# Attention logits from three bf16 parts instead of two fp32r parts, with the order of the stages set anew

## The chip, the cores and the metric

The kernel runs on one core of a Trainium2 chip. The metric is the device time of one execution in microseconds (us); a profiled execution of the same program gives the trace from which the views below are read. The engines are named as in the profile: PE is TensorE's matmul and PEld its weight load, DVE is VectorE, ACT is ScalarE, POOL is GpSimd, SP is SyncE, which issues most of the DMAs.

## What is computed

Two layers, each an attention with a compressive memory followed by a SwiGLU FFN, on 2048 rows of 512 numbers, in fp32. The reference, cut to the attention part that matters here:

```python
B, S, D = x.shape                      # 1, 2048, 512
H = 32; Dh = D // H; N = 4; L = S // N # 32 heads of 16, four segments of 512 rows
q, k, v = ...                          # x @ wq, x @ wk, x @ wv, as (B, H, N, L, Dh)
mask = (ar[:, None] < ar[None, :]) * (-1e9)
for s in range(N):
    qs, ks, vs = q[:, :, s], k[:, :, s], v[:, :, s]
    logits = jnp.einsum("bhqd,bhkd->bhqk", qs, ks) * scale + mask
    p = _softmax(logits, axis=-1)
    a_dot = jnp.einsum("bhqk,bhkd->bhqd", p, vs)
    ...                                # a_mem is read from M and z of the segments before
    o = g * a_mem + (1.0 - g) * a_dot
    ...                                # M and z take in this segment
return o @ wo
```

Each layer is x = x + attention(layernorm(x)), then x = x + FFN(layernorm(x)).

## The kernel before

**How the order is made.** The kernel doesn't issue as it goes. Every instruction is put on a list with its engine, an assumed cost, its readers and writers and a due time (`P.prio`), and `Program.issue` then plays the engines forward with these costs and always takes, among what is ready on an engine, what is due first. So the order on each engine's queue is fixed at build time, and on the chip each engine works its queue in that order and waits by semaphore. The constants at the top are the due times: `TA` and `TF` scale a unit of attention and a step of the FFN, `OFF` gives where within a unit each sort of work is spread, `PRE` the start of a layer, `EP`, `PAIR`, `STEP`, `WAT`, `TAT` and `FIN` the FFN.

**Precision.** A product of fp32 matrices is made from fp32r parts, high and low: three matmuls (`mm3`, line 282, for the projections) instead of one fp32 matmul of several passes. The logits do the same within one matmul: q and k have 16 numbers per head, and the three products (high by high, high by low, low by high) lie under each other in 48 rows of the contraction.

**A unit of attention** is one segment, one group of eight heads and one half of the group: four heads. There are 32 units per layer. For each unit:

- `qk_proj` (line 458, once for each tensor of a group) projects 128 columns of q or k, copies them out of PSUM (`raw`, line 468, ACT), rounds them to the high part (line 469, POOL), subtracts for the low part (line 471, POOL), and writes the parts to a scratch in DRAM with two DMAs (lines 483 and 484).
- `load3` (line 490) reads the scratch back with heads in another layout: `cq` with q's three rows of parts for each number and `ck` with k's, four DMAs of 192 KB per unit, issued by SP. Two heads lie in one contraction, in rows 0 to 47 and 64 to 111; `cq` is zero where the other head's rows are.
- `mx_units` (line 518) makes the row maxima. For each head and each block of 128 query rows one matmul of at least 256 key columns (line 531): 256 and 256 in one PSUM bank, 384 and 512 in one each; the ring of these banks, `pmx`, has two. DVE reduces each with the causal mask (line 538). A transpose (line 547), a negation (line 549, ACT) and a DMA of ACT's queue (line 550) put the negated maxima into row 127 of `cq`.
- `at_units` (line 559) makes the logits again, transposed, less the maximum: for each of ten blocks of 128 keys by 128 queries two matmuls of 256 columns (two heads each) into one bank of the ring `plt` of three (line 575); ACT takes the exponential (line 581); on the four diagonal blocks POOL zeroes the upper triangle (line 585). `pv` (line 603) multiplies by v in two steps, and `post` (from line 616) divides and writes the output.

Around these, matmuls of the projections, of the output `wo_proj`, of the memory (`mem_read`, `mem_update`) and the next segment's layernorm are spread. The FFN (lines 1005 and 1049 are its products) isn't touched except by the constants of its order.

## Time and profile before

| | us |
|---|---|
| three runs | 1931.92, 1933.54, 1934.31 |
| median of the runs | 1933.54 |
| span of the profiled execution, first to last instruction | 1931.2 |
| PE busy in the span | 1870.8 |
| DVE busy | 1406.9 |
| ACT busy | 873.0 |
| POOL busy | 905.9 |

The profiled execution has no time of its own beside its span, which lies 2.3 us under the median of the runs. A group's row reads: line, engine, operation, tiles written and read, shapes, count, then busy time, mean duration of one in ns, then the idle time of the engine just before such instructions and what ended most of it. In a timeline a row is start, duration, then the instruction. Busy time counts overlapping instructions of an engine once.

### The profile page before, as it was taken

What the parts mean: (1) busy time and instruction counts of PE and PEld (TensorE: products, weight loads), DVE (VectorE), ACT (ScalarE), POOL (GpSimd) and SP (SyncE); (2) the same over time, 40 slices, a digit from 0 to 9 for tenths busy, and PEclk for the clock granted to TensorE, in tenths of its full rate; (3) what the DMA queues carried; (4) which work ended last, traced back from release to release, by engine and by line L of the source; (5) the groups of instructions that cost most, each with busy time, mean ns of one, the idle gap of its engine ahead of it and who ended that gap; (6) DMA issues with size and microseconds to landing.
All of it is one profiled execution on the core that took longest, in us unless ns stands there. A gap on an engine that the chain in (4) does not pass through costs nothing.

```text
span 1931.2 us, 32319 instructions
## 1 busy us (share of the span) xinstructions
PE 1870.8 (97%) x11104; PEld 1437.2 (74%) x11104; DVE 1406.9 (73%) x3834; ACT 873.0 (45%) x1634; POOL 905.9 (47%) x1185
## 2 busy tenths in 40 slices
PE   7999999999989999999999999999999999999999
PEld 5677677776668887788867777777766788878887
DVE  5877867778777668766777678777797756686656
ACT  4555454555624343334326555555455334333332
POOL 5333443444546553655534334444355365455461
PEclk9999999999999999999999999999999999999999
DMA  7433434456131122221364344344561321221121
GB/s 235 135 111 124 132 116 146 129 151 195 45 136 50 55 72 82 71 61 44 95 215 121 102 133 132 116 149 132 152 188 39 131 66 44 87 77 51 44 60 44
DMA packets 120819, 206.09 MB, mean 107 GB/s; under 512 B 14160, under 2 KB 43856, under 8 KB 120656
## 3 DMA queue, kind: packets, MB, share of 16 engines
q1 hardware_dynamic: 118608, 203.49, 34.8%
q8 instruction: 89, 1.46, 0.3%
q10 hardware_dynamic: 2048, 0.53, 0.1%
q14 instruction: 74, 0.61, 0.1%
HBM read 136.34 MB, written 67.11 MB: 105 GB/s over the span
## 4 chain that ended last, share of the span: by engine, by line
PE 78%; DVE 8%; issue 4%; DMA 4%; POOL 3%; ACT 2%; SPq 0%; ACTq 0%; DVEq 0%; POOLq 0%
PE pj L282 16%; PE pj L1049 14%; PE plt L1005 11%; PE pmx L531 8%; PE pmx L1005 8%; PE ppv L603 7%; PE plt L575 6%; PE ppv L1005 3%; DVE junk L538 2%; DMA ck<-scrk 1%; PE pj L975 1%; PE pj L373 1%; PE pj L653 1%; DMA s<-nm 1%; POOL mem L858 1%
## 5 line engine op out<-in xcount | busy, mean ns | idle before, releaser
L538 DVE CUSTOM_DVE_ANT_0 junk<-pmx,amask 128x128 bf16<-128x128 f32 (+3 forms) x1024 | 458.7, 484 | 116.9 <-PE pmx L531 112.0
L282 PE MATMUL pj<-s,s 128*128 128x512 f32 x1416 | 488.2, 410 | 4.9 <-DVE s L1054 4.5
L1049 PE MATMUL pj<-s,vt 128*128 128x512 f32 x1296 | 414.4, 398 | 7.1 <-DVE s L1054 4.5
L581 ACT ACTIVATE s<-plt 128x512 f32<-128x512 f32 x512 | 284.2, 601 | 141.3 <-PE plt L575 133.3
L282 PEld LDWEIGHTS pj<-s,s 128*128 128x128 f32 x1416 | 263.9, 190 | 71.4 <-issue 24.9
L531 PE MATMUL pmx<-ck,s 127*128 127x256 f32 (+2 forms) x1024 | 299.1, 347 | 16.9 <-DVE mx L538 9.5
L1005 PE MATMUL plt<-s,s 128*128 128x512 f32 x1008 | 296.2, 396 | 3.4 <-ACT tt L1020 2.3
L1049 PEld LDWEIGHTS pj<-s,vt 128*128 128x128 f32 x1296 | 243.5, 189 | 68.9 <-DVE s L1054 8.0
L1054 DVE TENSOR_TENSOR s<-s,pj 128x512 f32<-128x512 f32 x224 | 152.9, 684 | 137.9 <-PE pj L1049 137.7
L575 PE MATMUL plt<-s,ck 128*128 128x256 f32 x1280 | 241.6, 288 | 4.2 <-DMA s<-nm 2.1
L531 PEld LDWEIGHTS pmx<-ck,s 127*128 127x128 f32 x1024 | 178.7, 190 | 88.8 <-DVE mx L538 27.0
L1005 PE MATMUL pmx<-s,s 128*128 128x512 f32 x720 | 239.2, 396 | 3.6 <-ACT s L871 2.4
L575 PEld LDWEIGHTS plt<-s,ck 128*128 128x128 f32 x1280 | 211.2, 189 | 32.7 <-ACT s L581 8.5
L1005 PEld LDWEIGHTS plt<-s,s 128*128 128x128 f32 x1008 | 189.6, 189 | 50.4 <-ACT tt L1020 2.7
L585 POOL TENSOR_SCALAR_AFFINE_SELECT s<-s 128x512 f32<-128x512 f32 x192 | 126.9, 664 | 186.5 <-ACT s L581 180.1
L1005 PEld LDWEIGHTS pmx<-s,s 128*128 128x128 f32 x720 | 135.5, 189 | 36.4 <-ACT s L871 3.2
L603 PE MATMUL ppv<-s,vt 128*32 128x512 f32 (+2 forms) x1536 | 136.8, 458 | 0.0
L872 POOL TENSOR_TENSOR s<-mem,s 128x512 fp32r<-128x512 f32 x96 | 126.4, 1318 | 0.0
L469 POOL TENSOR_SCALAR s<-raw 128x512 fp32r<-128x512 f32 x64 | 39.9, 624 | 181.0 <-ACT raw L468 180.6
L1005 PE MATMUL ppv<-s,s 128*128 128x512 f32 x288 | 112.8, 394 | 0.0
L879 POOL COPY turn<-vt 128x1 f32<-128x1 f32 x20 | 3.7, 184 | 230.0 <-DVE vt L962 230.0
L581 ACT ACTIVATE pc<-plt 128x512 f32<-128x512 f32 x128 | 76.8, 600 | 63.8 <-PE plt L575 62.5
(197 smaller groups left out, 2872.5 us busy)
## 6 DMA issues: line engine op xcount, KB each, us to landing
s<-scrq SPq DMA_DIRECT2D x128, 192.0 KB, 3.5
ck<-scrk SPq DMA_DIRECT2D x128, 192.0 KB, 4.5
scrq<-s SPq DMA_DIRECT2D x32, 512.0 KB, 3.0
scrk<-s SPq DMA_DIRECT2D x32, 512.0 KB, 3.1
scrq<-s SPq DMA_DIRECT2D x32, 256.0 KB, 2.0
scrk<-s SPq DMA_DIRECT2D x32, 256.0 KB, 2.0
xin<-xmid SPq DMA_DIRECT2D x32, 256.0 KB, 2.7
s<-xmid SPq DMA_DIRECT2D x32, 256.0 KB, 5.4
```

What stands on the lines that cost most here:

```text
L282: pe(n, passes, lambda: nc.tensor.matmul(view(ps.ap), lhsT=av(a.ap), rhs=bv(b.ap), start=start, stop=stop), [(a, rk[0]), (b, rk[1])], [ps])
L469: gp(0.59, lambda: nc.gpsimd.tensor_scalar(out=nat.ap[:, a, 0, :], in0=raw.ap, scalar1=1.0, scalar2=0.0, op0=OP.mult, op1=OP.add), [raw], ...
L531: nc.tensor.matmul(ps.ap[:, a * 256:a * 256 + nk], lhsT=cq.ap[0:127, 2 * j + p, qt * 128:(qt + 1) * 128], rhs=ck.ap[0:127, p, 0:nk], start ...
L538: dve(w, lambda a=a, qt=qt, w=w, ps=ps, junk=junk: nc.vector.tensor_tensor_reduce(out=junk.ap[:, :w], in0=ps.ap[:, a * 256:a * 256 + w], i ...
L575: nc.tensor.matmul(ps.ap[:, 256 * p:256 * p + 256], lhsT=ck.ap[:, p, kt * 128:kt * 128 + 128], rhs=cq.ap.rearrange("r (j p) c -> r p j c", ...
L581: act(512, lambda: nc.scalar.activation(Pb.ap[:, x].rearrange("p i c -> p (i c)"), ps.ap, AF.Exp, scale=SCALE), [ps], [(Pb, x)], table="exp")
L585: gp(0.593, lambda: nc.gpsimd.affine_select(out=Pb.ap[:, x], in_=Pb.ap[:, x], pattern=[[0, 4], [1, 128]], compare_op=OP.is_ge, fill=0.0, b ...
L603: nc.tensor.matmul(ps.ap[32 * i:32 * i + 32, q0:q0 + w], lhsT=vt.ap[:, kt, VW * hd:VW * hd + 32], rhs=f_[sl].ap[:, b0:b0 + w // 128, idx], ...
L872: gp(n / 400, lambda hi=hi, lo=lo, src=src: nc.gpsimd.tensor_sub(lo(), src(), hi().bitcast(F32)), [read, (wt, (o0, 0))], [(wt, (o0, 1))])
L1005: pe(512, 1, lambda i=i, kc=kc, x=x, buf=buf, view=view: nc.tensor.matmul(ps.ap, lhsT=w.ap[:, o, i, kc], rhs=view(buf.ap, kc), start=(x == 0),
L1049: pe(512, 1, lambda i=i, j=j, fi=fi, x=x, ps=ps, wt=wt, cs=cs: nc.tensor.matmul(ps.ap, lhsT=ht.ap[:, 0:2048].rearrange("p (f a c) -> p f a ...
L1054: dve(512, lambda ps=ps, t=t: nc.vector.tensor_add(xb.ap[:, t, :], xb.ap[:, t, :], ps.ap), [ps, (xb, t)], [(xb, t)])
```

## The change

q and k are each split into three bf16 parts instead of two fp32r parts: round to bf16 (POOL), subtract (POOL), round the rest (ACT), subtract again (POOL). Six products (every pair of parts but the three smallest) lie in 6 x 16 = 96 rows of the contraction, for one head per matmul; the scratch has six rows of parts, written in three DMAs, and `load3` has one DMA of 384 KB for q and one for k. The negated maximum is split into two bf16 parts as well, which go to rows 96 and 97 against rows of ones, with two DMAs. Since one head is one matmul, the columns are the exact causal widths: for the maxima 128, 256, 384 or 512 keys, packed to full banks (`MXB`, five banks for two heads); for the logits 512, 384, 256 or 128 queries (ten banks for four heads). The triangles are zeroed four heads at a time by `tri`, four instructions per unit as before, once all exponentials of the buffer's blocks are made. The planner's costs for the new matmuls count no weight load (`loads=0`). All constants of the order have new values, those of the FFN among them.

```diff
-PAIR, STEP, WAT, TAT = 13.0, 1.83, -2.5, (-1.0, -0.5)
+PAIR, STEP, WAT, TAT = 12.518, 2.534, -3.116, (-0.932, -0.425)
...
-FIN = 1.9
-WQ1 = -6.0
-TA, TF = 15.0, 16.7
-OFF = {'qe': (0.481, 1.468), 'at': (0.3, 1.1), 'mx': (-0.666, 0.16), 'lf': (-0.709, -0.318), 'mr': (0.865, 0.781), 'mu': (0.556, 0.139), 'wo': (0.263, 1.746), 'qk': (-0.342, 0.41), 'v': (-0.3, 0.518), 'lp': (0.034, 1.108)}
-PRE = {'c': -1.851, 'mb': 0.212, 'lv': -1.7, 'lo': -0.87, 'gate': -1.0, 'v': -1.534, 'dv': 0.12, 'qk1': -1.2, 'mx': -1.0}
-EP = {'w': -1.935, 'wn': 0.178, 'ln': -3.0, 'dn': -0.06, 'up': -2.73}
+FIN = 1.768
+WQ1 = -5.451
+TA, TF = 14.964, 15.962
+OFF = {'qe': (0.628, 1.66), 'at': (0.101, 1.238), 'mx': (-0.602, 0.614), 'lf': (-1.174, -1.011), 'mr': (0.951, 0.747), 'mu': (1.331, 0.736), 'wo': (-0.091, 1.887), 'qk': (0.072, 0.439), 'v': (-0.029, 1.348), 'lp': (0.034, 1.542)}
+PRE = {'c': -1.891, 'mb': -0.617, 'lv': -1.755, 'lo': -1.008, 'gate': -1.122, 'v': -1.534, 'dv': 0.401, 'qk1': -0.884, 'mx': -1.261}
+EP = {'w': -0.913, 'wn': 0.898, 'ln': -2.365, 'dn': -0.073, 'up': -4.471}
...
-                g["nat"] = sb(S8["nat"], [128, 2, 2, 512], F32R)
+                g["nat"] = sb(S8["nat"], [128, 8, 512], BF16)
...
-            gp(0.59, lambda: nc.gpsimd.tensor_scalar(out=nat.ap[:, a, 0, :], in0=raw.ap, scalar1=1.0, scalar2=0.0,
-                                                     op0=OP.mult, op1=OP.add), [raw], [(nat, (a, 0))])
-            gp(1.23, lambda: nc.gpsimd.tensor_sub(nat.ap[:, a, 1, :], raw.ap, nat.ap[:, a, 0, :].bitcast(F32)),
-               [raw, (nat, (a, 0))], [(nat, (a, 1))])
+            z = [a + (i if nm == "q" else 2 - i) for i in range(3)]
+            res = lambda: nat.ap[:, 6:8].rearrange("p a c -> p (a c)").bitcast(F32)
+            gp(0.61, lambda: nc.gpsimd.tensor_copy(nat.ap[:, z[0]], raw.ap), [raw], [(nat, z[0])])
+            gp(1.26, lambda: nc.gpsimd.tensor_sub(res(), raw.ap, nat.ap[:, z[0]]), [raw, (nat, z[0])], [(nat, "r")])
+            act(512, lambda: nc.scalar.copy(nat.ap[:, z[1]], res()), [(nat, "r")], [(nat, z[1])], sbuf=True)
+            gp(1.26, lambda: nc.gpsimd.tensor_sub(nat.ap[:, z[2]], res(), nat.ap[:, z[1]]),
+               [(nat, "r"), (nat, z[1])], [(nat, z[2])])
...
-            scr = P.buf(dram, "scr" + nm, [128, 3, 512], F32, ring=5)
-            r2, r1 = (0, 2) if nm == "q" else (1, 0)
-            dma(lambda: nc.sync.dma_start(scr.ap[:, r1], nat.ap[:, a, 0].bitcast(F32)), [(nat, (a, 0))], [(scr, r1)])
-            dma(lambda: nc.sync.dma_start(scr.ap[:, r2:r2 + 2], nat.ap[:, a].bitcast(F32)),
-                [(nat, (a, 0)), (nat, (a, 1))], [(scr, r2)], kb=512)
+            scr = P.buf(dram, "scr" + nm, [128, 6, 512], BF16, ring=5)
+            for d0, k0, k in ((5, z[0], 1), (3, min(z[:2]), 2), (0, a, 3)):
+                dma(lambda d0=d0, k0=k0, k=k: nc.sync.dma_start(scr.ap[:, d0:d0 + k], nat.ap[:, k0:k0 + k]),
+                    [(nat, e) for e in range(k0, k0 + k)], [(scr, d0)], kb=128 * k)
...
-                cq = sb(S8[f"c{u}"], [128, 4, 512], F32R)
-                ck = CK.get(u) or sb(f"ck{u}", [128, 2, 512], F32R)
-                C3[u] = cq, ck
+                C3[u] = cb = sb(S8[f"c{u}"], [128, 2, 4, 512], BF16)
                 pr, P.prio = P.prio, base + PRE["c"] * T
-                after = [XTL] if u else []
-                gp(0.9, lambda cq=cq: nc.gpsimd.memset(cq.ap[:, 0:2].bitcast(F32), 0.0), after, [(cq, 0)])
-                gp(0.9, lambda cq=cq: nc.gpsimd.memset(cq.ap[:, 2:4].bitcast(F32), 0.0), after, [(cq, 1), (cq, "m")])
-                if u not in CK:
-                    gp(0.9, lambda ck=ck: nc.gpsimd.memset(ck.ap.bitcast(F32), 1.0), after, [ck])
-                    CK[u] = ck
+                gp(1.8, lambda cb=cb: nc.gpsimd.memset(cb.ap[96:98, 1], 1.0), [XTL] if u else [], [(cb, "1")])
                 P.prio = pr
...
+            cb = C3[u % NB]
+            HLF[u] = {"c": cb}
+            for a, nm in enumerate("qk"):
+                dma(lambda a=a, nm=nm: nc.sync.dma_start(
+                    cb.ap[0:96, a], g["scr" + nm].ap.rearrange("(i h d) r c -> h (d r) i c", h=2, d=DH)[h]),
+                    [g["scr" + nm]], [(cb, a)], kb=384)
+
+        PARTS = (((0, 0, 512, 0, 0),), ((1, 128, 384, 1, 0), (3, 384, 128, 1, 384), (2, 256, 256, 2, 0)))
+        MXB = (((0, 0), (0, 2)), ((0, 3),), ((1, 0), (1, 2)), ((1, 3),), ((0, 1), (1, 1)))
...
-            def head(p, j):
+            def part(blocks):
                 def f():
...
+                    ps, offs, q0 = bank("pmx", ring=2), [], 0
+                    for i, qt in blocks:
+                        offs.append(q0)
+                        q0 += 128 * (qt + 1)
+
+                    def fill():
+                        for (i, qt), o in zip(blocks, offs):
                             w = 128 * (qt + 1)
-                            junk = sb("junk", [128, 512], BF16, ring=2)
-                            dve(w, lambda a=a, qt=qt, w=w, ps=ps, junk=junk: nc.vector.tensor_tensor_reduce(
-                                out=junk.ap[:, :w], in0=ps.ap[:, a * 256:a * 256 + w], in1=amask.ap[:, 512 - w:],
-                                scale=1.0, scalar=-3e38, op0=OP.add, op1=OP.max,
-                                accum_out=mx.ap[:, 2 * j + p, qt:qt + 1]),
-                                [(ps, a), amask], [junk, (mx, (qt, p, j))])
+                            nc.tensor.matmul(ps.ap[:, o:o + w], lhsT=cb.ap[0:96, 0, i, qt * 128:qt * 128 + 128],
+                                             rhs=cb.ap[0:96, 1, i, 0:w], start=True, stop=True)
+                    pe(512, 1, fill, [(cb, 0), (cb, 1)], [ps], loads=0)
+                    for (i, qt), o in zip(blocks, offs):
+                        w = 128 * (qt + 1)
+                        junk = sb("junk", [128, 512], BF16, ring=2)
+                        dve(w, lambda i=i, qt=qt, w=w, o=o, junk=junk: nc.vector.tensor_tensor_reduce(
+                            out=junk.ap[:, :w], in0=ps.ap[:, o:o + w], in1=amask.ap[:, 512 - w:],
+                            scale=1.0, scalar=-3e38, op0=OP.add, op1=OP.max,
+                            accum_out=mx.ap[:, i, qt:qt + 1]), [(ps, o), amask], [junk, (mx, (i, qt))])
                 return f
 
             def fin():
-                ps, nm = bank("pj"), sb("nm", [16, 128], F32R, ring=2)
+                ps, nm = bank("pj"), sb("nm", [16, 2, 128], BF16, ring=2)
                 pe(128, 2, lambda: nc.tensor.transpose(ps.ap[:16, 0:128], mx.ap.rearrange("p t h -> p (t h)"),
                                                        ident.ap), [mx, ident], [ps])
...
+                act(128, lambda: nc.scalar.mul(nm.ap[:, 0], ps.ap[:16, 0:128], -1.0), [ps], [(nm, 0)])
+                dve(128, lambda: nc.vector.scalar_tensor_tensor(out=nm.ap[:, 1], in0=ps.ap[:16, 0:128], scalar=-1.0,
+                                                                in1=nm.ap[:, 0], op0=OP.mult, op1=OP.subtract),
+                    [ps, (nm, 0)], [(nm, 1)])
+                for r in range(2):
+                    op("act", 0.1, lambda r=r: nc.scalar.dma_start(
+                        cb.ap[96 + r:97 + r, 0].rearrange("o x (t c) -> o (x t) c", t=4), nm.ap[:, r]),
+                        [(nm, r)], [(cb, f"m{r}")]).post = 2.2
+            parts = [[(i + x, qt) for x, qt in e] for i in (0, 2) for e in MXB]
+            return [part(e) for e in parts] + [fin]
...
-            def lt(kt, qt):
+            def lt(sl, x, blocks):
                 def f():
-                    b, x = BLOCKS[kt, qt]
-                    if b not in f_:
-                        f_[b] = sb(S8[f"p{b}"], [128, 4, 4, 128]) if b < 2 else sb("pc", [128, 2, 4, 128])
-                    Pb, ps = f_[b], bank("plt", ring=3)
+                    if sl not in f_:
+                        f_[sl] = sb(S8[f"p{sl}"] if sl < 2 else "pc", [128, 4, 512] if sl < 2 else [128, 2, 512])
+                    Pb, ps = f_[sl], bank("plt", ring=3)
 
                     def fill():
...
+                        o = 0
+                        for i, kt in blocks:
+                            w = 512 - 128 * kt
+                            nc.tensor.matmul(ps.ap[:, o:o + w], lhsT=cb.ap[0:98, 1, i, kt * 128:kt * 128 + 128],
+                                             rhs=cb.ap[0:98, 0, i, kt * 128:512], start=True, stop=True)
+                            o += w
+                    pe(512, 1, fill, [cb], [ps], loads=0)
+                    act(512, lambda: nc.scalar.activation(Pb.ap[:, x], ps.ap, AF.Exp, scale=SCALE), [ps], [(Pb, x)],
                         table="exp")
-                    if kt == qt:
-                        gp(0.593, lambda: nc.gpsimd.affine_select(
-                            out=Pb.ap[:, x], in_=Pb.ap[:, x], pattern=[[0, 4], [1, 128]], compare_op=OP.is_ge, fill=0.0,
-                            base=0, channel_multiplier=-1), [(Pb, x)], [(Pb, x)])
+                return f
+
+            def tri(sl, q0):
+                def f():
+                    Pb = f_[sl]
+                    k = 4
+                    v = lambda: (Pb.ap if sl < 2 else Pb.ap.rearrange("p a (b c) -> p (a b) c", b=2))[:, :, q0:q0 + 128]
+                    gp(0.593, lambda: nc.gpsimd.affine_select(
+                        out=v(), in_=v(), pattern=[[0, k], [1, 128]], compare_op=OP.is_ge, fill=0.0,
+                        base=0, channel_multiplier=-1), [Pb], [Pb])
...
+                                P_ = f_[sl].ap if sl < 2 else f_[sl].ap.rearrange("p a (b c) -> p (a b) c", b=2)
+                                nc.tensor.matmul(ps.ap[32 * idx:32 * idx + 32, q0:q0 + w],
                                                  lhsT=vt.ap[:, kt, VW * hd:VW * hd + 32],
-                                                 rhs=f_[sl].ap[:, b0:b0 + w // 128, idx], start=(k == 0),
+                                                 rhs=P_[:, idx, b0:b0 + w], start=(k == 0),
...
-            units = [lt(0, q) for q in range(4)] + [lt(1, q) for q in (1, 2, 3)] + [pv(0)]
-            units += [lt(2, 2), lt(3, 3), lt(2, 3), pv(1)]
-            units.append(post)
+            def both(*fs):
+                return lambda: [f() for f in fs]
+            A = [lt(0, i, ((i, 0),)) for i in range(4)]
+            B = [lt(1, i, ((i, 1), (i, 3))) for i in range(4)]
+            C = [lt(2, j, ((2 * j, 2), (2 * j + 1, 2))) for j in range(2)]
+            units = A[:3] + [both(A[3], tri(0, 0))] + B[:3] + [pv(0), both(B[3], tri(1, 0), tri(1, 384))]
+            units += [C[0], both(C[1], tri(2, 0)), pv(1), post]
```

53 lines of the change are left out of this document (4 added, 49 removed).

## The prediction

> **What bounds the kernel now.** I read the page first, then the stages, then the two attention lines, then a stretch of single instructions.
>
> ```profile
> span 1931.2 us, 32319 instructions
> PE 1870.8 (97%) x11104; PEld 1437.2 (74%) x11104; DVE 1406.9 (73%) x3834; ACT 873.0 (45%) x1634; POOL 905.9 (47%) x1185
> PE 78%; DVE 8%; issue 4%; DMA 4%; POOL 3%; ACT 2%; SPq 0%; ACTq 0%; DVEq 0%; POOLq 0%
> ```
>
> PE is busy 97% of the span and is 78% of the chain that ended last. So a microsecond taken off PE's stream is a microsecond off the end, unless another engine is next in that stage.
>
> ```profile
> core 0: us, PE busy (x) PEld busy (x) DVE busy (x) ACT busy (x) POOL busy (x), PEclk, DMA share, GB/s
> 0.00:66.00 66.00, 52.17 (x260) 38.77 (x264) 42.74 (x139) 29.01 (x53) 32.51 (x59) 0.95 0.66 206
> 66.00:523.00 457.00, 445.52 (x3404) 329.64 (x3392) 349.96 (x1304) 249.50 (x486) 198.85 (x300) 1.00 0.44 131
> 523.00:1027.00 504.00, 488.67 (x2138) 388.61 (x2135) 356.58 (x626) 185.15 (x328) 253.67 (x286) 0.99 0.28 86
> 1027.00:1480.00 453.00, 445.10 (x3421) 328.77 (x3419) 346.96 (x1286) 251.33 (x487) 199.68 (x303) 1.00 0.44 131
> 1480.00:1931.00 451.00, 439.38 (x1899) 351.38 (x1895) 310.64 (x480) 157.97 (x280) 221.18 (x237) 1.00 0.21 66
> ```
>
> The stages are: start; attention of layer 1; its FFN; attention of layer 2; its FFN. In both attentions PE is busy 97 to 98%. DVE has 107 us free there, ACT 207 and POOL 258. The clock is granted in full. But for the order, the change touches only attention, whose 64 units (32 per layer, four heads each) take some 14 us each.
>
> Busy time does not say how densely matmuls follow each other, since one starts before the last has ended. For that I read the starts. The first fence is PE, the second its weight loads.
>
> ```profile
> 200.14 0.40 PE L531 MATMUL pmx<-ck,s 127*128 127x512 f32 x1
> 200.38 0.40 PE L282 MATMUL pj<-s,s 128*128 128x512 f32 x1
> 200.61 0.40 PE L531 MATMUL pmx<-ck,s 127*128 127x256 f32 x2
> 200.85 0.40 PE L282 MATMUL pj<-s,s 128*128 128x512 f32 x1
> 201.08 0.39 PE L575 MATMUL plt<-s,ck 128*128 128x256 f32 x2
> 201.32 0.40 PE L282 MATMUL pj<-s,s 128*128 128x512 f32 x1
> ...
> 202.29 0.44 PE L531 MATMUL pmx<-ck,s 127*128 127x384 f32 x1
> 202.57 0.39 PE L282 MATMUL pj<-s,s 128*128 128x512 f32 x1
> ```
>
> ```profile
> 202.29 0.19 PEld L531 LDWEIGHTS pmx<-ck,s 127*128 127x128 f32 x1 [0.43 <-DVE mx L538]
> 202.40 0.19 PEld L282 LDWEIGHTS pj<-s,s 128*128 128x128 f32 x1
> ```
>
> A matmul of 512 columns is followed after 0.23 us (200.38 to 200.61; 200.85 to 201.08), two of 256 after 0.24 (201.08 to 201.32), 0.118 each. By the difference a column costs (0.232 - 0.118) / 256 = 0.445 ns, and 384 columns come to 0.175. The matmul at 202.29 was late: its weight load waited for DVE. Then 384 columns took 0.28, 0.10 over 0.175, because the load, normally done under the matmul before, stood in the open; the next load followed it after 0.11.
>
> **The change part by part.**
>
> *Matmuls.* Before, a unit has 16 matmuls for the maxima (eight of 256, four of 384, four of 512) and 20 of 256 for the logits: 28 x 0.118 + 4 x 0.175 + 4 x 0.232 = 4.93 us. After, each half has four each of 128, 256, 384 and 512: 32 matmuls, 10,240 columns for 10,752, in bf16. No matmul here has bf16 operands, so I bound it.
> - Upper end: a load takes 0.11 as in the fence, so one of 128 columns can't take less, and the rest costs what it does in f32: 8 x (0.11 + 0.118 + 0.175 + 0.232) = 5.08, **+0.15 per unit, +10 us** in 64.
> - Loads hidden, same fixed part: 128 columns take 0.061; 8 x 0.586 = 4.69, -0.24, -15 us.
> - Lower end: columns alone, 10,240 x 0.445 ns = 4.56, **-0.37, -24 us**.
>
> I take -24: fixed part and load length both hang on the weights, whose bytes are halved.
>
> On what a load costs, the Trainium skill's "TensorE: Matmul & The Clock Gate", section "Weight-path perf modes — Fast Weight Load (FWL) and DoubleRow", says that weights of 128 columns that are not FP32 are loaded over four paths, about twice as fast as measured there; no run here shows it so far. Its section "Back-to-back issue gap" puts a lone bf16 matmul at N/2.4 + 2.5 ns, an estimate by that page of 4.35 us per unit and -37 us in place of -24. The same section speaks against the change too: a stream in which each matmul of 128 columns has its own load runs at 81 ns, which would give back 8 x 25 ns x 64, 13 us of it.
>
> *Loads in the open.*
>
> ```profile
> L531 PE MATMUL pmx<-ck,s 127*128 127x256 f32 x512 | 110.3, 297 | 7.4 <-DMA ck<-scrk 5.0 <-DVE mx L538 0.8 <-DVE of L635 0.5
> L531 PE MATMUL pmx<-ck,s 127*128 127x512 f32 x256 | 109.9, 429 | 3.8 <-DVE mx L538 3.1 <-PE ppv L603 0.4
> L531 PE MATMUL pmx<-ck,s 127*128 127x384 f32 x256 | 93.8, 366 | 5.7 <-DVE mx L538 5.6
> L575 PE MATMUL plt<-s,ck 128*128 128x256 f32 x1280 | 241.6, 288 | 4.2 <-DMA s<-nm 2.1 <-ACT s L581 1.5
> L575 PE MATMUL plt<-s,ck x1280: 274/281/390, 57.4 to 1476.7; 128*128 128x256 f32 x183
> L1005 PE MATMUL ppv<-s,s 128*128 128x512 f32 x288 | 112.8, 394 | 0.0
> ```
>
> A matmul behind an open load is longer in the records (0.44 above). Those with nothing in the way take 281 ns at 256 columns (the median) and 394 at 512 (line 1005), so 337 at 384. The means lie 16, 35, 29 and 7 ns above: 512 x 16 + 256 x 35 + 256 x 29 + 1280 x 7 = 33.5 us of open loads and late clock. If the bf16 load is as long, nothing goes; if it vanishes, -33. I take half, **-17**. The groups that can wait fall from 22 to 20 per unit, a tenth of the other half, **-2**.
>
> *DVE.* The reductions keep their widths: per head 128, 256, 384 and 512. Added per unit is one subtraction on 16 x 128 for the second part of the negated maximum; DVE's nearest row is one of 128 x 34 at 184 ns, and ACT's same tile takes 257:
>
> ```profile
> L685 DVE TENSOR_TENSOR mtmp<-pj,bmask 128x34 f32<-128x34 f32 x24 | 4.4, 184 | 4.0 <-PE pj L681 3.9
> L549 ACT ACTIVATE nm<-pj 16x128 fp32r<-16x128 f32 x64 | 16.4, 257 | 21.8 <-PE pj L547 21.8
> L550 ACTq DMA_DIRECT2D s<-nm x64: 509/510/600, 54.0 to 1463.2; - x64
> L581 ACT ACTIVATE s<-plt 128x512 f32<-128x512 f32 x512 | 284.2, 601 | 141.3 <-PE plt L575 133.3
> L471 POOL TENSOR_TENSOR s<-raw,s 128x512 fp32r<-128x512 f32 x64 | 84.3, 1317 | 3.8
> L585 POOL TENSOR_SCALAR_AFFINE_SELECT s<-s 128x512 f32<-128x512 f32 x192 | 126.9, 664 | 186.5 <-ACT s L581 180.1
> ```
>
> That is 8 us per layer in 107 free: hidden. It delays its row by some 0.3 us; behind it on DVE stand other reductions, for which PE waits at line 531. If nothing covered it, 64 x 0.25 = +16.
>
> *ACT.* A second DMA for that row holds ACT's queue for 0.51 us (line 550; the planner books 0.1), and each of the 64 projections gets a copy of 512 (some 0.6). That is 1.1 per unit. Behind both are queued the exponentials, for which PE waits (three plt banks). Cover: ACT waits 133 us for line 575 in this row alone, 2.1 per unit. I take **0**; uncovered it is +70.
>
> *POOL.* Each projection gets one more subtraction of 1.32: +84 us in 516 free. The triangles stay four per unit but come after all four heads' exponentials, and the split goes POOL, ACT, POOL, so the triangles behind it, and the products with v behind these, can wait. Two layer ends have no other work to hide a triangle: **+1.4**.
>
> *DMA.* The bytes stay (768 KB written per tensor and group, 768 KB read per unit); SP issues 10 per group for 12. **0**, between -2 and +2.
>
> *Start.* The first q and k split gets ACT 0.6 and POOL 1.3 longer; the chain there runs on to k's load:
>
> ```profile
> 32.62 0.37 SPq L508
> ...
> 35.40 7.00 DMA ck<-scrk
> 42.53 0.77 PE pmx L531 x2
> ```
>
> The queue was at line 508 only at 32.6, behind another load, so part is hidden: **+2**, between 0 and +4.
>
> *Order.* The new constants move stages in all four parts, FFN included, and every DMA issued in them. They can win at most PE's idle 60 us (1931 - 1871), and lose about as much. By the rows each stage is already near full; I take **0**, ends -15 and +15.
>
> **Sum:** -24 - 17 - 2 + 1.4 + 2 = -40. The span of 1931.2 becomes 1891; the runs' median of 1933.54 lies 2.3 above the span, so **1894**.
>
> **The rivals.**
> - *Cheaper still:* matmuls at full clock with no fixed part and every load hidden. It speaks for this that weights have half the bytes, against it that the waits themselves stay. -24 - 33 - 2 + 3 = -56, and -15 from the order: 1862 at the far end, about 1873 in the middle.
> - *Loads hidden, but the fixed part and the open loads stay:* -15 - 2 + 3 = -14: 1919.
> - *Slower, the load bounds.* If a bf16 load takes 0.11, the matmuls cost +10, nothing of the open loads goes, start and ends cost 3.4: **1947**. It decides once a 128-column matmul takes over 0.11 - 10/512 = 0.09 us. For it: all full-width loads here follow at 0.11 at the best, whatever stands around them. Against: all of them are f32.
> - *The split stalls.* POOL and ACT hand over twice in each projection, and the engines issue in order. 64 times 0.8 us of PE waiting (two hand-overs' worth of a 0.6 copy behind an exponential) is 51 us, over the gain: 1945. Against it stands ACT's 2.1 us of waiting per unit and two units of lead of each projection.
> - *It does not do what it says:* the chip treats both types alike, and columns alone count: 512 x 0.445 ns x 64 = 15 us, the second rival's time.
>
> **How the numbers follow.** Forecast 0.45; cheaper still 0.22; fixed part stays 0.15; load bounds 0.09; split stalls 0.05; order or start eats the gain 0.04 (half of it within 0.2%, which is about what a measurement can tell from no change, 3.9 us, half slower). So faster 0.82, same 0.02, slower 0.16. The range leaves out the two slower cases and the far tail of the cheap one: 1862 to 1930.
>
> **What would show it.** For lines 531 and 575's successors: 512 columns at about 0.22, 128 at about 0.06 between starts, means of durations near their undisturbed ones. Attention spans of about 437 and 433 us for 457 and 453, FFN spans within a few us. DVE busy time there up by 8, POOL by 42 per layer. The prediction is wrong if 128-column matmuls are 0.11 apart, if PE waits for ACT's residual copy or POOL's triangles in the list of waits, or if FFN stages change by more than 15 us.

## The result, and the profile after

The changed kernel takes **1956.37 us** (median of four runs, 1955.81 to 1959.23) where the kernel before takes 1933.92 beside it: a ratio of 1.0113 [1.0101, 1.0126], 1.1% slower. The forecast was 1894, and the range ended at 1930. Size and sign were both wrong, so the question is where some 62 us went.

The page of the changed kernel, its first two rows and the chain that ended last:

```profile
span 1956.8 us, 31920 instructions
PE 1854.0 (95%) x10848; PEld 1269.5 (65%) x10848; DVE 1421.9 (73%) x3898; ACT 911.5 (47%) x1694; POOL 973.9 (50%) x1240
PE 73%; DVE 10%; issue 6%; DMA 6%; POOL 3%; ACT 2%; SPq 0%; ACTq 0%; DVEq 0%; POOLq 0%
```

PE is busy 17 us less than before and the span is 26 us longer: PE now stands idle 103 us, before 60. The chain has 73% of PE where it had 78, and more of DVE, of DMA and of "issue". No other engine is near full, so nothing became the bound by its amount of work. The same table of stages as before (span of the stage, then busy time of PE, PEld, DVE, ACT and POOL, granted clock, DMA share, GB/s):

```profile
66.00:524.00 458.00, 430.85 (x3243) 245.24 (x3242) 348.00 (x1314) 265.13 (x508) 220.10 (x319) 0.98 0.41 128
524.00:1040.00 516.00, 493.56 (x2150) 386.89 (x2148) 364.80 (x636) 189.00 (x337) 269.33 (x295) 0.99 0.27 85
1040.00:1494.00 454.00, 428.32 (x3279) 244.43 (x3271) 347.83 (x1312) 265.56 (x509) 221.05 (x324) 0.98 0.42 130
1494.00:1956.00 462.00, 448.61 (x1926) 358.67 (x1918) 314.25 (x489) 159.12 (x282) 227.34 (x245) 0.99 0.21 65
```

The attentions took 458 and 454 us instead of the forecast 437 and 433, although PE is busy 15 to 17 us less in each, and the FFN stages grew by 12 and 11. A part of that growth is only moved: 40 early FFN matmuls of 0.233 us (line 971), 9 us, left the attention stages. PE's list of waits (total, times, longest) shows the first thing that is new:

```profile
PE plt L565 <- DMA s<-nm: 22.4, 14, 3.0
PE pmx L522 <- DVE mx L528: 16.1, 45, 1.5
PE pj L373 <- DVE s L378: 7.5, 3, 3.4
```

The rows that answer to the first two in before's list:

```profile
PE pmx L531 <- DVE mx L538: 9.5, 23, 1.1
PE plt L575 <- DMA s<-nm: 2.1, 3, 1.0
```

The logits' matmuls wait 22.4 us for the negated maxima where they waited 2.1, and those of the maxima wait 16.1 for DVE where they waited 9.5.

**Reading the matmuls themselves.** In these groups the mean duration grew for the projections, though they are the same matmuls:

```profile
L282 PE MATMUL pj<-s,s 128*128 128x512 f32 x1416 | 529.1, 467 | 2.5 <-DVE s L1050 1.2 <-DVE s L378 0.6 <-DVE mem L657 0.4
L565 PE MATMUL plt<-s 98*128 98x512 bf16 x256 | 92.1, 398 | 23.6 <-DMA s<-nm 22.4 <-ACT pc L569 0.7 <-ACT s L569 0.2
L522 PE MATMUL pmx<-s 96*128 96x128 bf16 x256 | 58.5, 229 | 10.7 <-DVE mx L528 6.8 <-DMA s<-scrk 3.4
L565 PEld LDWEIGHTS <-s 98*128 98x128 bf16 x1024 | 83.3, 100 | 121.1 <-issue 81.0
```

A projection has a mean of 467 ns for 410. That is no cost by itself: in a mixed stream a matmul's record starts early, while the one before is still running. Starts therefore mislead here, and I read the ends (start plus duration; the profiler models the ends of matmuls). A stretch of PE:

```profile
177.33 0.53 PE L282 MATMUL pj<-s,s 128*128 128x512 f32 x1
177.70 0.83 PE L565 MATMUL plt<-s 98*128 98x384 bf16 x6
```

The projection ends at 177.86 and the six logit matmuls behind it (three of 384 and three of 128 columns; a row carries the shape of its first) end at 178.53. That is 0.22 us for each 384 and 128 together. Over all matmuls of the trace, bf16 behind bf16 ends 56, 110, 163 and 217 ns (medians) after the one before for 128, 256, 384 and 512 columns, and the first one behind an fp32r matmul 16 ns later. The Trainium skill's "TensorE: Matmul & The Clock Gate", section "Back-to-back issue gap", gives N/2.4 + 2.5 ns for a lone matmul, and that agrees (56 and 217 here); its 81 ns for a stream of 128 columns with their loads does not appear here. The bf16 load's record is 100 ns, the f32 ones' 189.

With the ends of all matmuls, each put down to its kind, the whole span can be accounted for (us; the 11 missing to the span are 7 up to the end of the first matmul and 4 behind the last). The two columns in the middle are experiments explained below, in which the second part of the maximum is left out:

| matmuls | before | second part out, order of before | second part out, order of after | after |
|---|---|---|---|---|
| maxima | 215.7 | 193.8 | 183.9 | 186.1 |
| logits | 166.1 | 156.9 | 158.2 | 183.0 |
| of these two, time above the usual spacing | 63.3 | 58.3 | 49.9 | 73.3 |
| projections (line 282) | 382.6 | 386.9 | 386.3 | 389.4 |
| FFN products | 898.3 | 905.0 | 908.0 | 910.1 |
| products with v | 155.4 | 161.4 | 159.6 | 160.7 |
| layernorm's transposes | 36.0 | 39.5 | 46.3 | 47.0 |
| all others | 66.0 | 66.3 | 69.5 | 69.2 |
| sum | 1920.1 | 1909.8 | 1911.8 | 1945.5 |

"Usual spacing" is the median of the kind and width. Without what lies above it, maxima and logits went from 318.5 to 295.7 us: **-23**. What lies above it went up by 10, and all the other matmuls, which the change did not touch, by 38.

### The profile page after: what moved, and what is told of

The parts are those of the page before. It is cut to its first block, busy times and chain, and to the rows that moved or that the text cites. A ratio compares the mean times of both kernels' runs of the same rounds, so it can differ in the third digit from the quotient of the medians.

```text
span 1956.8 us, 31920 instructions
## 1 busy us (share of the span) xinstructions
PE 1854.0 (95%) x10848; PEld 1269.5 (65%) x10848; DVE 1421.9 (73%) x3898; ACT 911.5 (47%) x1694; POOL 973.9 (50%) x1240
## 4 chain that ended last, share of the span: by engine, by line
PE 73%; DVE 10%; issue 6%; DMA 6%; POOL 3%; ACT 2%; SPq 0%; ACTq 0%; DVEq 0%; POOLq 0%
PE pj L282 15%; PE pj L1045 14%; PE plt L1001 10%; PE pmx L1001 8%; PE ppv L595 6%; PE plt L565 6%; PE pmx L522 6%; PE ppv L1001 3%; DMA s<-nm 3%; DVE junk L528 3%; PE pj L971 2%; POOL mem L854 1%; PE plt L971 1%; PE pj L373 1%; POOL s L868 1%
## 5 line engine op out<-in xcount | busy, mean ns | idle before, releaser
L282 PE MATMUL pj<-s,s 128*128 128x512 f32 x1416 | 529.1, 467 | 2.5 <-DVE s L1050 1.2
L522 PE MATMUL pmx<-s 96*128 96x384 bf16 (+3 forms) x1024 | 248.6, 309 | 20.8 <-DVE mx L528 16.1
L565 PE MATMUL plt<-s 98*128 98x512 bf16 (+3 forms) x1024 | 233.5, 310 | 25.1 <-DMA s<-nm 22.4
L522 PEld LDWEIGHTS <-s 96*128 96x128 bf16 x1024 | 81.3, 100 | 137.3 <-issue 117.7
L565 PEld LDWEIGHTS <-s 98*128 98x128 bf16 x1024 | 83.3, 100 | 121.1 <-issue 81.0
L469 POOL CAST s<-raw 128x512 bf16<-128x512 f32 x64 | 40.4, 632 | 164.2 <-ACT raw L466 155.5
L472 POOL TENSOR_TENSOR s<-s 128x512 bf16<-128x512 f32 x64 | 76.6, 1197 | 48.0 <-ACT s L471 47.7
```

What stands on the lines that cost most here:

```text
L282: pe(n, passes, lambda: nc.tensor.matmul(view(ps.ap), lhsT=av(a.ap), rhs=bv(b.ap), start=start, stop=stop), [(a, rk[0]), (b, rk[1])], [ps])
L472: gp(1.26, lambda: nc.gpsimd.tensor_sub(nat.ap[:, z[2]], res(), nat.ap[:, z[1]]), [(nat, "r"), (nat, z[1])], [(nat, z[2])])
L522: nc.tensor.matmul(ps.ap[:, o:o + w], lhsT=cb.ap[0:96, 0, i, qt * 128:qt * 128 + 128], rhs=cb.ap[0:96, 1, i, 0:w], start=True, stop=True)
L565: nc.tensor.matmul(ps.ap[:, o:o + w], lhsT=cb.ap[0:98, 1, i, kt * 128:kt * 128 + 128], rhs=cb.ap[0:98, 0, i, kt * 128:512], start=True, st ...
```

## The experiments

The theory after this reading was that the second part of the maximum lengthens the chain ahead of the logits, and that the new order, which puts the maxima later, leaves no room for it. The rivals: the constants of the order cost the time by themselves, whatever the arithmetic; the bf16 matmuls give nothing; the FFN's order lost it.

### The two halves of the change apart

```diff
 # new_math_old_order: the changed kernel ...
-TA, TF = 14.964, 15.962
+TA, TF = 15.0, 16.7
...
 # old_math_new_order: the kernel before ...
-TA, TF = 15.0, 16.7
+TA, TF = 14.964, 15.962
...
```

All constants of the order were exchanged in each, those of the front's diff.

> The bf16 logits with all constants of the order as before. Theory 'order': the new constants cost the FFN its 12.5 and 11.4 us, so these stages go back to some 504 and 451 us and the whole to about 1932; attention stays near 457 and 454. Rival 'fitted': the new constants belong to the new matmuls, and with the old ones the logits wait longer still: 1956 or more, with attention over 460.

> The fp32r logits with all constants of the order as in the changed kernel. Theory 'order': the FFN stages grow by some 12 us each as in the changed kernel, 1950 to 1960. Rival 'the math': if the FFN's loss came in by what attention leaves behind (buffers, early work), the FFN stays near 504 and 451 and the whole near 1934.

Measured: the new arithmetic in before's order 1930.82, ratio 0.9981 [0.9972, 0.999]; the old arithmetic in the new order 1956.63, ratio 1.0115 [1.0098, 1.0132]. So the arithmetic alone gains 3 us, not 40, and the constants cost 23 on the old arithmetic and 26 on the new. The order was a loss on both, but the waits that grew differ. Of old_math_new_order, the wait of the logits and the stages:

```profile
PE plt L575 <- DMA s<-nm: 8.0, 7, 2.5
```

```profile
67.00:524.00 457.00, 440.47 (x3381) 326.40 (x3374) 342.90 (x1293) 250.19 (x483) 192.51 (x292) 1.00 0.44 129
524.00:1034.00 510.00, 491.90 (x2149) 390.88 (x2151) 361.74 (x633) 185.52 (x330) 263.14 (x294) 0.99 0.28 86
1034.00:1496.00 462.00, 446.28 (x3425) 327.97 (x3417) 342.62 (x1287) 253.37 (x485) 195.83 (x301) 1.00 0.43 129
1496.00:1954.00 458.00, 442.24 (x1913) 353.81 (x1903) 313.86 (x483) 159.57 (x281) 223.86 (x239) 0.99 0.21 65
```

With one row of maxima the same wait is 8.0 us instead of 22.4, and the loss is spread over the last three stages by 6 to 9 us each, at nearly full clock.

### The second part of the maximum, in a fixed order

When an instruction is removed from the list, the planner makes another order, and that alone moves the time. So in these kernels the second part, or half of it, stays on the list with its cost and isn't issued. In the traces of the three in the changed kernel's order, all 10848 matmuls stand in the same sequence as in the changed kernel. Left out of the computation is the second part (row_out_same_order, row_out_old_order and subtract_only don't use it, second_dma_only sends zeros in its place). The negated maximum is then rounded to bf16; the softmax is unchanged by it, since the same shift is taken from a whole row.

```diff
 # row_out_same_order; row_out_old_order has before's constants as well
-                dve(128, lambda: nc.vector.scalar_tensor_tensor(out=nm.ap[:, 1], in0=ps.ap[:16, 0:128], scalar=-1.0,
-                                                                in1=nm.ap[:, 0], op0=OP.mult, op1=OP.subtract),
-                    [ps, (nm, 0)], [(nm, 1)])
+                dve(128, lambda: None, [ps, (nm, 0)], [(nm, 1)])
...
-                        cb.ap[96 + r:97 + r, 0].rearrange("o x (t c) -> o (x t) c", t=4), nm.ap[:, r]),
+                        cb.ap[96 + r:97 + r, 0].rearrange("o x (t c) -> o (x t) c", t=4), nm.ap[:, r]) if r == 0 else None,
...
-                            nc.tensor.matmul(ps.ap[:, o:o + w], lhsT=cb.ap[0:98, 1, i, kt * 128:kt * 128 + 128],
+                            nc.tensor.matmul(ps.ap[:, o:o + w], lhsT=cb.ap[0:97, 1, i, kt * 128:kt * 128 + 128],
 # subtract_only: only the last two edits
 # second_dma_only: the first edit, and zeros that are ready from the start for the second DMA
-                        cb.ap[96 + r:97 + r, 0].rearrange("o x (t c) -> o (x t) c", t=4), nm.ap[:, r]),
+                        cb.ap[96 + r:97 + r, 0].rearrange("o x (t c) -> o (x t) c", t=4), nm.ap[:, r] if r == 0 else zrow.ap),
```

> The changed kernel with the second part of the negated maximum planned but not issued: the order of everything else stays as it was, only the DVE subtraction and the second DMA are gone (97 rows). Theory 'row': the two instructions themselves cost, by ACT's queue and the later row, so most of the 38.7 us between the changed kernel and the one with one maximum row goes here too: 1917 to 1930. Rival 're-planned': that gain came from another order of everything, and with the same order under 12 us go: 1944 to 1956.

> The changed kernel's order, with the DVE subtraction for the second part but without its DMA (97 rows; the second part isn't used). Of the 29 us that the subtraction and the DMA cost together: theory 'DMA queue' (the second DMA waits on ACT's queue for DVE and holds the exponentials, and the logits wait for the later row) gives under 8 us to the subtraction alone, 1925 to 1934; rival 'DVE' (the subtraction delays the reductions) gives it most, 1942 to 1954.

> The changed kernel's order, without the subtraction; the second DMA sends zeros that stand ready, so it follows the first one without a wait for DVE, and row 97 adds nothing. Theory 'DMA queue, its 0.51 us': 10 to 20 us of the 29 remain, 1937 to 1947. Rival 'hand-over': what costs is ACT's wait for DVE between the two DMAs, and with zeros ready under 8 us remain, 1925 to 1934.

> The bf16 logits in the order of before, with the second part planned but not issued, as in the run with the changed kernel's order. Theory 'lead': with 1.14 units of lead the later row costs less, so under 12 us go from 1931: 1919 to 1929. Rival 'queue': the two instructions cost ACT and DVE the same time in any order, so some 29 us go: about 1902.

Measured, against before:

| | second part not issued | second part issued |
|---|---|---|
| before's constants | 1925.01, 0.9956 [0.994, 0.9973] | 1930.82, 0.9981 [0.9972, 0.999] |
| new constants | 1927.2, 0.9963 [0.9949, 0.9976] | 1956.37, 1.0113 [1.0101, 1.0126] |

This table is the core of the case. The second part costs 6 us in before's order and 29 in the new one; the new constants cost 2 us (within the uncertainty) without it and 26 with it. With the bf16 arithmetic neither is slow by itself: the loss is the two together. Of the 29, the subtraction alone is 2 (subtract_only 1929.48, 0.9975 [0.9965, 0.9985]), the second DMA alone, with its data ready, 22.5 (second_dma_only 1949.71, 1.0082 [1.0067, 1.0097], more than the 10 to 20 us that its theory allowed); the rest, 4 to 5 us, comes when both are there and the DMA waits for DVE.

The logits' waits of three kernels, row_out_same_order, second_dma_only and new_math_old_order, to set beside the 22.4 of after:

```profile
PE plt L563 <- DMA s<-nm: 4.0, 4, 2.1
```

```profile
PE plt L564 <- DMA s<-zrow: 16.4, 13, 3.4
```

```profile
PE plt L565 <- DMA s<-nm: 3.1, 4, 1.3
```

The same wait falls with the row and falls with the order. What it consists of, from the tile `nm` of the changed kernel (duration min, median, max in ns, first and last start):

```profile
L543 ACTq DMA_DIRECT2D s<-nm x128: 510/511/1565, 50.8 to 1477.2; - x128
L538 ACT ACTIVATE nm<-pj x64: 248/251/268, 50.5 to 1476.1; 16x128 bf16<-16x128 f32 x64
L539 DVE SCALAR_TENSOR_TENSOR nm<-pj,nm x64: 236/274/279, 51.1 to 1476.9; 16x128 bf16<-16x128 f32 x64
...
DMA to landing us min/median/max: 1.6/1.7/5.7
```

Each DMA holds ACT's queue for 0.51 us and lands 1.7 us (median) after its issue began, at most 5.7. From the end of the maxima's transposition to the end of the last DMA's issue it is 2.17 us on average in after, 1.23 with one row, 1.21 before. The room for that chain is the time from the transposition to the unit's first logit matmul: 8.0 us (median) before, 7.5 for the new arithmetic in before's order, 5.2 in after. With 7.5 us the second part hardly shows in this wait (3.1 us, 4 times); with 5.2, 14 of the 64 units wait.

Which units wait goes with the landing. In those 14 the slower of the two rows landed 4.6 us (median) after its issue began, in the other 50 after 1.8; in 9 of the 14 the first row had landed within 1.8 us and only the second was late. Rows that took more than 2.5 us to land met DMA engines that were busy for 0.55 of the 1.5 us after the issue, the others 0.22. One unit, in order of issue:

```profile
325.89 0.51 ACTq L543 DMA_DIRECT2D s<-nm  x1
327.38 0.38 SPq L501 DMA_DIRECT2D s<-scrq  x1
327.56 0.27 DVE L539 SCALAR_TENSOR_TENSOR nm<-pj,nm 16x128 bf16<-16x128 f32 x1
327.80 0.54 SPq L501 DMA_DIRECT2D s<-scrk  x1
327.86 0.51 ACTq L543 DMA_DIRECT2D s<-nm  x1
```

The first row landed after 1.7 us. The subtraction came late on DVE, two loads of the scratch were issued meanwhile, the second row landed after 5.6, and the logits waited 2.43 us for it. So the second row costs more than its 0.51 us where it meets the loads of the scratch. That the loads delay it is read from these times; no run moved them.

One such place in the changed kernel, a timeline (start, duration, instruction, idle time before it and what ended it):

```profile
256.43 0.27 PE L536 MATMUL pj<-ident,mx 128*16 128x128 f32 x1
256.89 0.25 ACT L538 ACTIVATE nm<-pj 16x128 bf16<-16x128 f32 x1
257.17 0.28 DVE L539 SCALAR_TENSOR_TENSOR nm<-pj,nm 16x128 bf16<-16x128 f32 x1 [3.68 <-ACT nm L538]
257.27 1.16 ACTq L543 DMA_DIRECT2D s<-nm  x2
259.85 0.61 PE L595 MATMUL ppv<-pc,vt 128*32 128x256 f32 x8
263.45 1.44 PE L565 MATMUL plt<-s 98*128 98x512 bf16 x3 [2.98 <-DMA s<-nm]
```

and the same unit in row_out_same_order, first the row, then both kernels' windows around it, after's first:

```profile
260.03 0.82 PE L563 MATMUL plt<-s 97*128 97x512 bf16 x3 [2.06 <-DMA s<-nm]
```

```profile
257.00:263.00 6.00, 3.47 (x34) 1.96 (x32) 2.77 (x6) 3.20 (x6) 4.35 (x6) 0.96 0.81 226
263.00:269.00 6.00, 5.55 (x15) 3.07 (x15) 1.03 (x4) 2.17 (x4) 0.39 (x1) 0.50 0.27 106
```

```profile
257.00:263.00 6.00, 3.94 (x35) 2.16 (x27) 3.14 (x8) 3.42 (x7) 2.50 (x3) 1.00 0.89 281
263.00:269.00 6.00, 6.00 (x35) 3.34 (x38) 5.64 (x27) 2.61 (x6) 1.40 (x3) 1.00 0.00 1
```

The third column from the end is the granted clock. After the wait of 2.98 it is 0.50 for the six microseconds that follow, in which 15 matmuls pass; in the other kernel it is 1.00 after the wait of 2.06, and 35 pass (not all of the same widths). So this late row is paid twice: once as the wait, once as half a clock behind it. Two waits are no threshold, though. In the changed kernel's trace a wait of 1.83 us that ended at 1531.3 was followed by half clock, and one of 2.49 that ended at 1237.1 was not:

```profile
1531.00:1536.00 5.00, 4.74 (x14) 3.77 (x15) 4.83 (x8) 0.62 (x1) 0.00 (x0) 0.66 0.68 257
1237.00:1244.00 7.00, 6.92 (x37) 4.24 (x37) 4.38 (x21) 3.29 (x6) 0.69 (x2) 1.00 0.35 120
```

The mean granted clock of after and of row_out_same_order:

```profile
core 0: 1956.8 us, clock 0.980
```

```profile
core 0: 1923.2 us, clock 0.989
```

2.0% of 1956.8 is 39 us, 1.1% of 1923.2 is 21: by this estimate at most 18 of the 33.6 us between these two spans are half clock, since PE also idles in it. The pair is not typical: the granted clocks of all runs of the two kernels have medians of 0.9835 and 0.988, which makes it some 9 of the 29 us. "TensorE: Matmul & The Clock Gate", Part 1, has the Trainium skill's account of it: an idle window of about 3.4 us halves the clock. The trace agrees that it is a halving and not a slope (its granted values are 1.0 and 0.5 alone), and shows it after waits shorter than that, 2.98 and 1.83 us.

### Can the order be mended by its constants?

```diff
 # old_ffn_order: the changed kernel, before's values of
+PAIR, STEP, WAT, TAT = 13.0, 1.83, -2.5, (-1.0, -0.5)
+FIN = 1.9
+TA, TF = 14.964, 16.7
+EP = {'w': -1.935, 'wn': 0.178, 'ln': -3.0, 'dn': -0.06, 'up': -2.73}
 # old_lead: the changed kernel; in OFF
-'at': (0.101, 1.238), 'mx': (-0.602, 0.614)
+'at': (0.3, 1.1), 'mx': (-0.666, 0.16)
 # short_lead_old_math: the kernel before; in OFF the reverse
 # true_dma_cost: the changed kernel
-                    op("act", 0.1, lambda r=r: nc.scalar.dma_start(
+                    op("act", 0.51, lambda r=r: nc.scalar.dma_start(
```

> The changed kernel with only the constants of the FFN (PAIR, STEP, WAT, TAT, FIN, EP, TF) as before. Theory 'order': the FFN stages are back at 504 and 451, attention as in the changed kernel or some 4 us longer each (the early FFN matmuls come back into it): 1932 to 1940. Rival 'attention's end': the FFN's loss comes from the constants of attention or from the math, and the time stays at 1950 or more.

> The changed kernel with the due times of the maxima and of the logits ('mx' and 'at' of OFF) as before, which puts the last maxima 1.14 units ahead of the first logits for them instead of 0.49. Theory 'lead': the logits wait because the row is made too late, so attention gets shorter by 10 to 20 us in all and the list of waits loses the 22 us on the row: 1936 to 1946. Rival: the lead isn't it, the time stays within 4 us of 1956.

> The changed kernel with the planner told that a DMA issued by ACT takes 0.51 us of its queue instead of 0.1. Theory 'row': much of the loss is that everything behind the two DMAs on ACT comes later than planned; with the true cost the order allows for it: 1930 to 1945. Rival 'lead': the due times leave too little room whatever the planner knows: 1950 to 1960.

> The kernel before with only the due times of maxima and logits ('mx' and 'at') of the changed one, 0.49 units of lead instead of 1.14. Theory 'lead': most of the 22.7 us that the whole new order cost the old matmuls, 12 to 22 us, is here: 1946 to 1956. Rival: the loss is spread over the other constants, under 6 us here: 1934 to 1940.

- old_ffn_order: 1953.8, 1.0095 [1.0078, 1.0111]. The FFN stages shrink by 13.7 and 8.6 us, the attentions grow by 8.5 and 8.8, since the early FFN matmuls move back into them. Most of the FFN's growth was moved work; 3 us are left to this rival, where 16 to 24 were expected.
- short_lead_old_math: 1945.76, 1.006 [1.0045, 1.0076]. The two due times of the maxima and the logits cost 11 to 12 us, about half of the 23 of all constants, even with one row; that is at the edge of what the theory 'lead' allowed.
- old_lead: 1954.12, 1.0105 [1.0088, 1.0122]; true_dma_cost: 1949.8, 1.008 [1.0065, 1.0096]. Giving the lead back, or telling the planner what the DMA really holds, recovers 2 and 7 us of 29. That is a miss for the plain form of the theory. Both kernels are planned anew, so they have another order throughout and not after's with a longer lead. In old_lead's trace the lead is back at 7.7 us, the logits wait 7.8 us for the row instead of 22.4 and take 171.4 us by the ends instead of 183.0; but the matmuls under "all others" take 81.3 instead of 69.2. So the lead did shorten this wait, and the new order lost most of the gain elsewhere.

### One row for the maximum, planned as such

```diff
 # one_max_row: the changed kernel; one_row_old_order has before's constants as well
-                ps, nm = bank("pj"), sb("nm", [16, 2, 128], BF16, ring=2)
+                ps, nm = bank("pj"), sb("nm", [16, 128], BF16, ring=2)
...
-                act(128, lambda: nc.scalar.mul(nm.ap[:, 0], ps.ap[:16, 0:128], -1.0), [ps], [(nm, 0)])
+                act(128, lambda: nc.scalar.mul(nm.ap, ps.ap[:16, 0:128], -1.0), [ps], [nm])
...
-                for r in range(2):
+                op("act", 0.1, lambda: nc.scalar.dma_start(
+                    cb.ap[96:97, 0].rearrange("o x (t c) -> o (x t) c", t=4), nm.ap), [nm], [(cb, "m0")]).post = 2.2
```

> The changed kernel with the negated maximum as one bf16 row instead of two parts (the rounding shifts all logits of a row alike, so softmax keeps its value): no DVE subtraction, one DMA of ACT's queue, 97 rows. Theory 'row': the logits' waits for that row, 22 us on PE by the list of waits, fall to the 2 to 5 us of before, and 10 to 20 us go: about 1940. Rival 'order': the row is late because the order places it late, whatever is in it; under 5 us go, 1952 to 1956.

> One maximum row as in the run before, with all constants of the order of before. If the order's loss and the second row's add up, 1931 less some 15 to 35: 1896 to 1916. If they are the same loss (a late row, by little lead or by more work), the two together give no more than the better one: 1915 to 1925.

Measured: 1917.68, 0.9915 [0.9898, 0.9933], and 1937.79, 1.0015 [1.0002, 1.0029]. These do the same work as row_out_same_order (1927.2) and row_out_old_order (1925.01); only the planner knows that the second part is gone. Once this gains 9.5 us, once it loses 12.8; neither time lies in an expected range. So a new plan of the same work is worth about 10 us either way, and an experiment that lets the planner run again can't settle a few microseconds.

### The narrow matmul last in its bank

The ends show one price that the forecast did not have. Behind a logit bank of 384 and 128 columns, of 256 and 256, and of the same 384 and 128 in the other order; the first fence is the changed kernel, the second narrow_first:

```profile
254.75 0.85 PE L282 MATMUL pj<-s,s 128*128 128x512 f32 x3
255.44 0.39 PE L565 MATMUL plt<-s 98*128 98x384 bf16 x2
255.64 0.48 PE L282 MATMUL pj<-s,s 128*128 128x512 f32 x1
255.96 0.39 PE L565 MATMUL plt<-s 98*128 98x256 bf16 x2
256.11 0.47 PE L282 MATMUL pj<-s,s 128*128 128x512 f32 x1
```

```profile
249.72 0.53 PE L282 MATMUL pj<-s,s 128*128 128x512 f32 x1
250.09 0.39 PE L560 MATMUL plt<-s 97*128 97x128 bf16 x2
250.18 0.53 PE L282 MATMUL pj<-s,s 128*128 128x512 f32 x1
```

The ends in the first are 255.60, 255.83, 256.12, 256.35, 256.58. The projection behind the 128-column matmul takes 0.29, the one behind 256 columns 0.23: its own load of 0.11 has only 0.055 us of matmul to hide behind. There are some 120 such places in the changed kernel and 83 in before's order, 0.05 each. In the second fence the ends are 250.25, 250.48, 250.71, so 0.23 behind the 384.

```diff
 # narrow_first: one_max_row, in the same order of instructions; the same edit on row_out_old_order
 # is narrow_first_old_order
-                        o = 0
-                        for i, kt in blocks:
+                        ends = [sum(512 - 128 * kt for _, kt in blocks[:x]) for x in range(len(blocks))]
+                        for o, (i, kt) in sorted(zip(ends, blocks), key=lambda e: -e[1][1]):
...
-                            o += w
 # narrow_first_true_dma: narrow_first, planned with
-                op("act", 0.1, lambda: nc.scalar.dma_start(
+                op("act", 0.51, lambda: nc.scalar.dma_start(
```

> The kernel with one maximum row (1917.7) in the same order, but of the two logit matmuls in a bank the one of 128 columns goes before the one of 384. Theory 'open load': an fp32r matmul right behind 128 bf16 columns comes 0.05 us late because its load takes 0.11; some 121 such places in the changed kernel, so 4 to 8 us go: 1910 to 1914. Rival 'waits only': PE has slack there anyway and the time stays within 2 us of 1917.7.

> The same swap in the order of before with the second row planned but not issued (1925.0). Theory 'open load': 1917 to 1921. Rival 'waits only': 1923 to 1927.

> One maximum row, narrow matmul first, and the planner told 0.51 us for the remaining DMA of ACT's queue, which orders everything anew. Theory 'true price': the row's DMA already costs 0.51 that the plan doesn't know, so the plan gets better, 1900 to 1912. Rival 'any new order moves the time by some 10 us either way': anywhere from 1903 to 1925.

Measured: narrow_first **1913.1, 0.9875 [0.9859, 0.9892]**, for one_max_row's 0.9915; narrow_first_old_order 1922.19, 0.9927 [0.9908, 0.9946], for 0.9956. That is 6 to 8 us by the ratios (3 to 5 by the medians, but before's own median was 2 to 3 us higher in this group of runs), where 120 times 0.05 is 6 and 83 times 0.05 is 4. The intervals of the first pair just part, those of the second overlap, and 1922.19 lies between its two expectations. In the traces the projections take 385.8 us by the ends for 391.7 in the first pair, and 383.7 for 386.9 in the second. narrow_first is the best version here, 1.2% faster than before. narrow_first_true_dma is 1922.78, 0.9928 [0.9908, 0.9948]: the truer cost made the plan 10 us worse, another new plan of the same work.

## Why the prediction was wrong, step by step

- **Matmuls, -24: right in size, partly by luck.** Their usual spacing fell by 23 us (318.5 to 295.7); 128 columns follow at 0.056, so the rivals "the load bounds" (0.11) and "both types alike" are out. But the step let the fixed part vanish and kept 0.445 ns a column. Measured behind one another, the 32 bf16 matmuls of a unit take 4.37 us for the 4.56 forecast, -36 us in 64 units against the 4.93 of before. The 16 ns more behind an fp32r matmul, some 800 times, give 13 of it back, and the forecast had neither.
- **Open loads, -17 and -2: wrong.** In before's order, without the second part, the time above the usual spacing fell by 5 us (63.3 to 58.3), in after it rose by 10. The loads did get shorter (100 ns for 189), so their length was not most of that time. The step took all that the mean durations had above the undisturbed ones as loads in the open and halved it; part of it is waiting for DVE's reductions, which grew (9.5 to 16.1 us in the lists of waits).
- **Not in the sum: the neighbours.** All other matmuls take 21 us more in before's order without the second part (1538.3 to 1559.1 in the table's lower five kinds) and 38 more in after. The forecast took untouched lines as untouched. Shown of this are the loads behind narrow matmuls (4 us in before's order, 6 in after's) and the half clock of the later waits, which stretches whatever runs behind them: by the granted clock, 0.988 for 0.994, an estimate of 10 us at the most in before's order. The layernorm's transposes wait 7.5 us for line 378 in the new order. The rest of the 21 (projections 4, products with v 6, FFN 7) is not taken apart. An fp32r matmul of 512 columns ends some 5 ns later behind a bf16 one than behind another fp32r one (236 for 231), but no run removed that.
- **DVE, hidden: right.** The subtraction by itself is 2 us.
- **ACT, 0: the step that failed.** "Cover: ACT waits 133 us for line 575" counted the 0.51 us as occupancy of ACT's queue. ACT had the time, but the DMA's end was on the path: the logits can't start until the last row has landed. Its issue ended 0.9 us later on average, and where it met the loads of the scratch it landed several microseconds late. The right cover to look at was the lead of the maxima over the logits, and that lead was 8.0 us before and 5.2 after the change, whose own constants cut it: the due time of the maxima's end went from 0.16 to 0.614 of a unit and that of the logits' start from 0.3 to 0.101. Price in this order: 29 us for 0.
- **Order, 0 with ends of 15: wrong in kind.** It was priced by itself, and as such 2 us is what it cost without the second part. With it, 26, and on the old arithmetic 23, both beyond its end. An end of 15 for an order and a 0 for an added step in a chain don't bound the two together.
- **POOL and the split of q and k: right, or nearly.** The list of waits has no row of PE for the residual copy; for the triangles it has 2 us at the products with v and 14 at their weight loads, which run beneath the matmul before. POOL's busy time rose by 68 us (905.9 to 973.9) for the 84 forecast. **Start, +2:** it did not come; the first logits start at 53.6 us, before at 57.4.

The sum after the fact, from the medians: -9 for the arithmetic in before's order without the second part (by the account of the ends -26 matmuls, -5 open loads, +21 neighbours, so -10), +2 for the order, +29 for the second part in it: 1956. So of the 62 us between forecast and result, 29 are the second part and 2 the order with it left out; 31 were already missing from the arithmetic, most of them the neighbours and the open loads. What stays open: why the constants cost 23 us on the old arithmetic, of which the two due times explain half (by the ends, 14 lie in the maxima, 8 in the FFN and 7 in the layernorm's transposes, and the projections give 7 back); the split of the neighbours' 21 us; and whether after's order with a longer lead and nothing else changed would give the 29 us back, since every kernel with another lead was also planned anew. Both parts of the maximum in one DMA were not tried.

## What to carry to other kernels

An instruction that an idle engine issues is free only if its result is early; before it is priced at nothing, measure the lead of the chain that it lengthens, in the order that the change will have. A change of arithmetic and a change of order have to be priced together as well as apart: here the second part cost 6 us in the old order, the new order 2 us without it, and the two together 31. And where PE is dense, a wait of 2 to 3 us can cost up to twice its length, since half clock may follow it.

## What the runs showed of the hardware beside that

- An fp32r matmul of 512 columns follows a bf16 one of 128 columns after 0.28 to 0.29 us instead of 0.23, which fits its weight load (0.11 in the open) being longer than the 0.056 it can hide behind. With the narrow matmul first in its bank it was 0.23 again, behind 384 columns.
- The first bf16 matmul behind an fp32r one ends 16 ns later than one behind another bf16.
- A record of a matmul can start early when the type changes, so that projections "last" 467 ns for 410 at the same pace; ends tell the pace.
- PE waits of 1.83 and 2.98 us were followed by a clock of 0.50, waits of 2.06 and 2.49 were not; the stretches at half clock in the changed kernel last 3.4 to 10.2 us.
- A small DMA (4 KB) held ACT's queue for 0.51 us and landed 1.6 to 5.7 us after its issue began; the late ones met DMA engines more than twice as busy.
